# A list-scheduled attention and feed-forward kernel: other latency constants in its planner, and the tile table and side positions found under them

## The chip, the cores and the metric

The kernel runs on one core of one Trainium2 chip. The metric is the device time of one execution in microseconds (us): the median of several runs. Engines are named as the profile names them: PE (TensorE, matrix products), PEld (its weight loads), DVE (VectorE), ACT (ScalarE), POOL (GpSimd), SP (SyncE, which here issues the DMAs).

## What is computed

One layer-normalised input of 2048 rows by 512 columns goes through attention with 32 query heads of 16 columns and one shared key and value head, and in parallel through a feed-forward layer with GELU; both are added to the input.

```python
xn = _layernorm(x, axis=-1)
# attention: 32 heads, one k and one v head of 16 columns
scores = jnp.einsum("bhqd,bkd->bhqk", q, k) * (Dh ** -0.5)
p = _softmax(scores, axis=-1)
o = jnp.einsum("bhqk,bkd->bhqd", p, v)
# feed-forward: 512 -> 1792 -> 512
h = _gelu(jnp.einsum("bsd,df->bsf", x, w1) + b1)
return x + _A_ref(xn, ...) + _B_ref(xn, ...)
```

## The kernel before

**Tiles.** The score matrix is cut into 2048 tiles of 128 keys by 512 queries (one head each). Three tiles are a unit; there are 683 units. A unit's scores are made by PE in three of six PSUM banks (`scores`, L947); units alternate between the two halves of these six banks. Each tile then gets its exponential in one of two ways, and the string `DTAB` (L60) has one letter for each unit that says which of its three tiles goes which way.

- An exponential tile: ACT computes exp from PSUM into the buffer E (L970), one instruction for all such tiles of the unit, and PE multiplies it with V in one product (`pv_mm`, L1014).
- A spline tile: DVE makes a first pass from PSUM, add and max, into 16-bit integers Dt (L1001), whose bits read as bfloat16 are already a rough exponential. Three more shifted copies are made from it: two fast DVE instructions (L1047), the first over the batch, the second over twice the batch, and an in-place step of its own for each tile (L1044), which runs on POOL or on DVE. PE multiplies all five versions with V, so such a tile costs five products.

Spline tiles are collected in batches of one to six before the L1047 and L1044 steps. The letters `o`, `t`, `A`, `B`, `X` close the batch behind their unit; `0`, `2`, `a`, `b`, `x` do the same split without closing; `.` gives all three tiles to ACT. A batch also closes at six tiles and at the last spline tile of a group of 64.

**Other work.** Beside the units run the projections of the queries, the hidden layer of the feed-forward part (56 groups of products, evacuated by DVE at L1150), two GELU stretches on ACT (L1162, at units 182 and 512), the output products (`mm4`, L661) and the normalisation of the attention's output. `HP` and `YP` (L73, L74) hold the unit from which on each hidden group and each output tile may be planned.

**The planner.** Nothing of this order is written out by hand. The kernel first lists its operations with what they read and write, an assumed time on the engine (`occ`) and an assumed latency until another engine can go on (`lat`). `schedule` (L224) then plays all engines forward in time at build time and picks, for each engine that comes free, the ready operation with the earliest due time: that gives the fixed order of instructions of each engine. Waits between engines are semaphores, put in by `emit`; the planned times themselves don't reach the chip. `settle` (L457) works the times of the finished order out once more, and `emit` uses them to sort the waits of one instruction.

A POOL step has a rule of its own. DVE's fast operations (those marked `lock`) and POOL's are kept apart in the plan: when DVE starts an operation of at least `PL_WIN` (0.4) that isn't a fast one, a waiting POOL step may be placed in it, if POOL comes free within `PL_GATE` (0.1) of its start. The step is planned from `PL_START` after that start, lasts `PL_OCC` (0.62), can be used `PL_LAT` after its end, and fast DVE operations are barred until `PL_FREE` before its end:

```python
po.start = max(tt + PL_START, po.rdy, free["pool"])
po.end = po.start + po.occ
po.vis = po.end + po.lat
free["pool"] = tt = po.end
lockend = po.end - PL_FREE
```

A step that has been ready for `PL_TAKE` (1.0) may be taken by DVE instead, in its order of due times. `S_LAT` is the latency behind scores; DVE operations had 0.16, matrix products 0.23, exponentials 0.22.

Of the kernel before, what the change touches and what calls it, by code (L numbers as in the profile page):

```python
# [33 lines left out]
S_WAIT = 0.1  # L34
P_WAIT = 0.0
PL_OCC = 0.62
PL_LAT = 0.2
PL_GATE = 0.1
PL_WIN = 0.4
PL_TAKE = 1.0  # L40
PL_DUE = 3.0
PL_START = -0.07
PL_SEM = 0.16
PL_FREE = 0.135
NE_ND_KB = (23, 19, 11, 6)
LA = 34
LB = 120
# [9 lines left out]
DMASK = {".": (), "0": (0,), "2": (2,), "a": (0, 1), "b": (1, 2), "x": (0, 1, 2),  # L57
         "o": (0,), "t": (2,), "A": (0, 1), "B": (1, 2), "X": (0, 1, 2)}
CLOSE = "otABX"
DTAB = "t2t22t00202t..22tt..022.to00.t22t00200..o.t..20222o.o2.tot22.2t.t2222tt22..2o222t2..o202o02tt2.o.2.t0.t202.2.20t0toto.2..0ot.t2..ot0o2t02t.2222o.0t...o0ot2020o2.2t0.02.t00.02.20o002..xxXaoto.02oot.0to2tt.0too0.ot0tot.o0o020t0o0.tt20.t22.o0tto..2t2to220oo.22t0.2ooo.o2t2o.0ot0o.t02t022.to0..oot.2t2t.o0002ot.0.2tto.0tt2.02t0.202t.2t.oo.ot0.00t.t0o0.0o0o..o0o22o2.00.t0tot2.0o2.2o.t2o2o.tt22o.0t.0oo.2ot2t2.o0.t0t20to2.2t0t.tt2t.002tt.oo.o0oooo0.2o0o0.t00t2ot2.0t0tt0.oA.o..020tt2t02..t0000...2o..02ot0020o.t2t...00XbXttto200t.tt0o22tt..0t0t222.o2o2.t2t20.t0t0.t0t00t2o.0tt2tot.t000202t2t.o.0to20.0.2o22t0o.2t00o0t0..t02o0.0o.o0ooto.t2t0to.2oo0o222o0022o00.2t.2..t0t2.2t.tttt2.2.to.o.."  # L60
YF = 664
Y_ALLOW = 8.0
H_ALLOW = 5.0
YT_ALLOW = (3,3,3,3)
WF_ALLOW = 1.5
QP_ALLOW = 1.5
S_LAT = 0.27
S_REAL = 0.222
EXP_OCC = 0.0133
EXP_LAT = 0.16  # L70
Q3 = (7, 4, 2)
QK = ((48,88.7,157.4),(45,107.7,130.4),(62,118.7,159.4))
HP = ((14.33,26.29,49.54,147.27,14,38.77,51.6,14,34.61,92.18,56.17,130.88,103.7,49),(108.69,82.59,66.39,104.08,133,93.7,109.35,162.93,173.36,139,171.29,159.02,133,137.17),(308.62,328.89,290.1,325,306.98,336.81,316.24,310.73,293.91,381.46,369.7,349,374.48,453.6),(475,473.57,427,468.62,459.3,464.72,451,455.66,491.16,486.09,482.33,480.6,464.72,461.37))  # L73
YP = ((195.26,184.23,228.93,254.61),(353.39,411.43,387.54,421),(516,530.79,566.23,553.42),(600.53,607,655.32,660.47))  # L74
GU = ((182, (0, 1)), (512, (2, 3)))
FG = 7
UB2 = 2
# [13 lines left out]
NVA = 14  # L91
# [5 lines left out]
TBW = 512  # L97


def vcost(n, mode=1):  # L100
    return n / 0.96e3 / mode + 0.065
# [7 lines left out]
class Prog:  # L109
# [114 lines left out]
    def schedule(self):  # L224
# [17 lines left out]
        mode = None  # L242
# [6 lines left out]
        pend = 0.0  # L249
# [4 lines left out]
                accn[g] = accn.get(g, 0) + 1  # L254
        started = {}
        opened = None
        lockend, gate, prev = 0.0, None, None
        s_seen = False
        vleft = sum(op.kind == "v" for op in ops)
# [6 lines left out]
        while left:  # L266
# [11 lines left out]
            e, t = best_e, best_t  # L278
            cand = [o for o in able[e] if seen(o) <= t + 1e-9]
            if e == "pe":  # L280
                op = self.pick_pe(t, cand, ready["pe"], mode, visit, cgbusy)
# [8 lines left out]
                if op is None and self.pro_filler and not s_seen and low:  # L290
# [8 lines left out]
                    pend = st + f.occ  # L299
                    mode = "full"  # L300
# [13 lines left out]
                if FILL_GAP and tgt and low and st > FILL_FROM and lim - st > FILL_GAP:  # L314
# [12 lines left out]
                    pend = st + f.occ  # L327
                    mode = "col"
# [3 lines left out]
                if op == "idle":  # L332
                    op = None
# [4 lines left out]
            else:  # L338
                op = min(cand, key=self.due)
# [25 lines left out]
                if e == "dve" and op.kind == "pl":  # L365
                    ready["pool"].remove(op)
                    ready["dve"].append(op)
                    op.eng = op.stream = "dve"
                    op.kind, op.occ, op.lat = "post", vcost(TBW, 4), 0.16
                if e == "dve":  # L370
                    if op.lock:
                        gate = prev if prev is not None and t <= prev.end + 0.03 else op
# [7 lines left out]
            if e == "pe":  # L380
# [3 lines left out]
                if op.kind in ("pv", "side"):  # L384
                    cg = op.tag[1]
# [9 lines left out]
                    mode = "col"  # L395
                    g = op.tag[0]
                if op.kind == "pv":
                    n = accn[g] = accn[g] - 1
# [7 lines left out]
                elif op.kind != "side":  # L406
                    m = {"S": "row", "side": "col"}.get(op.kind, "full")
                    w = SWITCH if m != mode else 0.0
# [8 lines left out]
                    mode = m  # L417
# [4 lines left out]
            if e == "pe":  # L422
                while op.start > wend:
                    slow = 1.0 if area > HAM_T * WIN else 2.0
                    ncold += slow > 1
                    self.log.append((wend - WIN, area / WIN, slow))
                    area, wend = 0.0, wend + WIN
                pend = op.start + op.occ * slow
            free[e] = max(free[e], op.end)
            if op.pm:  # L430
                pmev = op if e == "dve" else None
# [5 lines left out]
            for o, cross in op.outs:  # L437
                o.nun -= 1
                v = op.vis if cross else op.end
# [8 lines left out]
        for op in order:  # L448
            if op.kind == "pv":
                g, cg, first = op.tag  # L450
# [5 lines left out]

    def settle(self):  # L457
        free = {e: 0.0 for e, _ in self.SECTIONS}
        mode, cg, pend = None, [0.0] * 4, 0.0
        for op in self.ops:  # L460
            occ = op.occ + EXP_OCC * (op.kind == "exp")
            lat = {"exp": EXP_LAT, "S": S_REAL, "fill": 0.0}.get(op.kind)
            lat = op.lat if lat is None else lat
            t = max([free[op.eng]] + [o.real for o in op.deps])
            if op.eng == "pe":
                if op.kind in ("pv", "side") or (op.kind == "fill" and occ > 0.15):
                    t = max(t, cg[op.tag[1]]) if mode == "col" else max([t, pend + SWITCH] + [c + SWITCH for c in cg])
                    cg[op.tag[1]] = t + 0.216
                    mode, end = "col", t + 0.006
                else:  # L470
                    m = "row" if op.kind == "S" else "full"
                    w = SWITCH if m != mode else 0.0
                    t = max([t, pend + w] + [c + w for c in cg])
                    mode, end = m, t + occ
                pend = t + occ
            else:
                end = t + occ
            free[op.eng] = max(free[op.eng], end)
            op.real = t + occ + lat

    def emit(self):
        self.settle()
# [44 lines left out]
def bass_parallel_sum__grouped_kv_mqa__dense_activation_gelu__prompt_kernel(  # L527
# [15 lines left out]
    S, D = xf.shape  # L543
# [17 lines left out]
    with ExitStack() as es:  # L561
# [76 lines left out]
        add = pr.add  # L638

        def B(b):  # L640
            return ("bank", b)

        def dve(fn, r=(), w=(), n=TBW, mode=1, allow=1.0, lat=0.16, **kw):
            return add("dve", fn, r, w, occ=vcost(n, mode), lat=lat, allow=allow, **kw)

        def act(fn, r=(), w=(), n=TBW, allow=0.0, lat=0.22, **kw):
            return add("act", fn, r, w, occ=0.051 + n / 1.2e3, lat=lat, allow=allow, **kw)
# [1 line left out]
        def mm(o, l, rh, start, stop, r=(), w=(), tp=None, skip=False, occ=0.216, allow=1.5, **ak):  # L649
            kw = {}  # L650
            if tp is not None:
                kw["tile_position"] = tp
            if skip:
                kw["skip_group_check"] = True
            return add("pe", lambda e: e.matmul(o, l, rh, start=start, stop=stop, **kw), r, w, occ=occ, lat=0.23,  # L655
                       allow=allow, **ak)

        def mm4(o, l, rh, start, stop, r=(), w=(), allow=1.5, **ak):
            for j in range(4):
                c = slice(32 * j, 32 * j + 32)  # L660
                add("pe", lambda e, c=c, j=j: e.matmul(o[c, :], l[:, c], rh, start=start, stop=stop,  # L661
                                                       tile_position=(0, 32 * j)),
                    r, [(k, j) for k in w] + [k for k in w if k != B(7)], occ=0.216, lat=0.23, allow=allow, kind="side", tag=(None, j), **ak)

        M4 = [(("bank", 7), j) for j in range(4)]

# [5 lines left out]
        for i in range(8):  # L672
            e = X_Q[i]
            dma("sp" if e == "s" else "act", x_sb[:, 2 * i:2 * i + 2, :], x_view[:, 2 * i:2 * i + 2, :], f"d_x{i}",
                w=[("x", 2 * i), ("x", 2 * i + 1)], lat=X_LAT[i], due=0.0)
# [6 lines left out]
        def setup(fn, r=(), w=(), occ=0.16, due=0.0, lat=0.1, **kw):  # L682
# [18 lines left out]
              w=[(k, g, j) for k in ("QT", "QTm") for g in range(NGR) for j in range(HG)])  # L701
        setup(lambda e: e.tensor_copy(wkp[:, :, :, 0:Dh], wvk[:, :, Dh:2 * Dh].unsqueeze(2).to_broadcast([P, DT, 4, Dh])),
              r=["wk_s", "wkp"], w=["wkp"], occ=0.35, due=2.0)
# [8 lines left out]
              r=["mrow"], w=["isc"], due=10.0)  # L712
# [10 lines left out]
        for gl in range(2):  # L723
            setup(lambda e, gl=gl: e.tensor_copy(sel_diag[gl], mask8[:, 4 * gl:4 * gl + 4].unsqueeze(1).to_broadcast([P, NGR // 2, HG])),
                  r=["mask8", "sel8"], w=["sel8"], due=12.0)
# [207 lines left out]
        def scores(u):  # L933
            ts = list(range(3 * u, min(3 * u + 3, NTILE)))
            x = u % 2
            pieces, r = [], []
            for i, t in enumerate(ts):
                gg, kt, j = tile_of(t)
                tb, g = divmod(gg, NGR)
                q0 = 32 * j  # L940
                pieces.append((bank(3 * x + i), KT[q0:q0 + 32, kt * P:(kt + 1) * P], QT[q0:q0 + 32, g, :], q0))
                r.append(("KT", kt))
                r += [k for k in q_rows(g) if k not in r]

            def fn(e):
                for o, l, rh, q0 in pieces:
                    ins = e.matmul(o, l, rh, start=True, stop=True, tile_position=(q0, 0))  # L947
                return ins
            return add("pe", fn, r, [B(3 * x + i) for i in range(len(ts))], occ=0.216, lat=S_LAT, allow=-1.0, kind="S")

# [62 lines left out]
        def pv_mm(gg, j, v, kt, rhs, r):  # L1013
            add("pe", lambda e, a, b: e.matmul(pO[32 * j:32 * j + 32, :], V1[:, v, kt, :], rhs, start=a, stop=b,  # L1014
                                               tile_position=(0, 32 * j)),
                r=r + [("V", v, 0 if kt < NVA else NVA)], acc="O", occ=0.216, lat=0.23,
                allow=4.0 if gg < NTB * NGR - 1 or kt < NT - 4 else -5.0, kind="pv", tag=(gg, j))

        def close_batch():
# [198 lines left out]
        side = []  # L1218
# [40 lines left out]
        for t in range(NTILE):  # L1259
            if is_d[t]:  # L1260
                first, n = (t, 1) if n == 0 else (first, n + 1)
                if n == KB or last_d[t // TPG] == t or (DTAB[t // 3] in CLOSE and not any(is_d[t + 1:t // 3 * 3 + 3])):
                    bsize[first], n = n, 0

        scores(0)
        scores(1)
        for u in range(NU):
# [89 lines left out]
```

## Time and profile before

| what | value |
|---|---|
| median of 3 runs | 750.98 us (750.9 to 751.15) |
| the profiled execution | 750.71 us |
| its span in the profile | 749.0 us |
| PE, DVE, ACT busy | 98% each |
| POOL busy | 364.4 us, 49% |
| first first-pass and first exponential start | 24.09 us |
| last exponential starts | 738.61 us |
| TensorE clock granted | 0.998 |

A row of the profile's groups reads: line, engine, operation, output and input with their shapes, count, then busy time and the mean of one instruction, then the engine's idle time ahead of such instructions and what ended it. The share of busy time is an average over records, and a record of DVE or ACT runs on while the next instruction has begun: to see how long an instruction holds its engine, one takes the distance from its start to the next one's.

### The profile page before, as it was taken

What the parts mean: (1) busy time and instruction counts of PE and PEld (TensorE: products, weight loads), DVE (VectorE), ACT (ScalarE), POOL (GpSimd) and SP (SyncE); (2) the same over time, 40 slices, a digit from 0 to 9 for tenths busy, and PEclk for the clock granted to TensorE, in tenths of its full rate; (3) what the DMA queues carried; (4) which work ended last, traced back from release to release, by engine and by line L of the source; (5) the groups of instructions that cost most, each with busy time, mean ns of one, the idle gap of its engine ahead of it and who ended that gap; (6) DMA issues with size and microseconds to landing.
All of it is one profiled execution on the core that took longest, in us unless ns stands there. A gap on an engine that the chain in (4) does not pass through costs nothing.

```text
span 749.0 us, 21922 instructions
## 1 busy us (share of the span) xinstructions
PE 732.8 (98%) x9046; PEld 228.2 (30%) x9046; DVE 736.1 (98%) x1436; ACT 733.2 (98%) x744; POOL 364.4 (49%) x506
## 2 busy tenths in 40 slices
PE   7999999999999999999999999999999999999998
PEld 4323222222233323232222222332233333322223
DVE  8899999999999999999999999999999999999996
ACT  8999999999999999999999999999999999999995
POOL 5443654343523576554546555553452466454441
PEclk9999999999999999999999999999999999999999
DMA  9200100000011011100101010100100101010101
GB/s 315 61 15 17 32 9 17 24 11 21 6 36 25 9 39 30 24 23 16 26 13 28 17 38 19 29 24 16 25 15 22 40 6 41 23 39 10 25 22 37
DMA packets 32077, 23.34 MB, mean 31 GB/s; under 512 B 16369, under 2 KB 27498, under 8 KB 31978
## 3 DMA queue, kind: packets, MB, share of 16 engines
q1 hardware_dynamic: 30922, 21.90, 10.9%
q8 instruction: 72, 1.18, 0.7%
q14 instruction: 27, 0.22, 0.1%
q10 hardware_dynamic: 1056, 0.03, 0.1%
HBM read 13.08 MB, written 2.35 MB: 21 GB/s over the span
## 4 chain that ended last, share of the span: by engine, by line
PE 40%; DVE 30%; ACT 28%; DMA 0%; issue 0%; SPq 0%
ACT E L970 28%; PE pAll L1014 19%; DVE Dt L1001 13%; PE pAll L947 13%; DVE Dt L1047 10%; PE pAll L661 7%; DVE x_sb L1150 2%; DVE stats L748 1%; DVE Dt L1044 1%; DVE Of L1059 1%; PE pAll L655 1%; DMA x_sb<-in_A_x_dram 0%; DVE oTp L1086 0%; DVE qp L1122 0%; DVE x_sb L1196 0%
## 5 line engine op out<-in xcount | busy, mean ns | idle before, releaser
L970 ACT ACTIVATE E<-pAll 128x1024 bf16<-128x1024 f32 (+1 forms) x678 | 682.4, 1226 | 1.7 <-PE pAll L947 1.2
L1044 POOL TENSOR_SCALAR Dt<-Dt 128x512 int16<-128x512 int16 x451 | 348.2, 772 | 360.6 <-DVE Dt L1047 143.8
L1014 PE MATMUL pAll<-Dt,V 128*32 128x512 bf16 x2775 | 421.8, 383 | 0.6 <-DVE Dt L1047 0.2
L1001 DVE TENSOR_SCALAR Dt<-pAll 128x512 int16<-128x512 f32 (+1 forms) x542 | 364.1, 688 | 1.0 <-PE pAll L947 0.8
L1047 DVE TENSOR_SCALAR Dt<-Dt 128x1024 int16<-128x1024 int16 (+7 forms) x548 | 288.0, 551 | 0.2
L1014 PE MATMUL pAll<-E,V 128*32 128x512 bf16 x1493 | 284.8, 385 | 0.2
L947 PE MATMUL pAll<-QT,KT 32*128 32x512 bf16 x2048 | 267.2, 384 | 6.2 <-ACT E L970 2.1
L947 PEld LDWEIGHTS pAll<-QT,KT 32*128 32x128 bf16 x2048 | 67.3, 91 | 279.5 <-ACT E L970 251.4
L1014 PEld LDWEIGHTS pAll<-Dt,V 128*32 128x32 bf16 x2775 | 110.9, 94 | 119.4 <-issue 72.0
L661 PE MATMUL pAll<-xnT,w_sb 128*32 128x512 bf16 x896 | 122.2, 383 | 0.4 <-DVE x_sb L1150 0.3
L1014 PEld LDWEIGHTS pAll<-E,V 128*32 128x32 bf16 x1493 | 65.9, 94 | 47.5 <-issue 34.7
L661 PE MATMUL pAll<-w_sb,x_sb 128*32 128x512 bf16 x448 | 69.3, 383 | 0.0
L661 PE MATMUL pAll<-w_sb,ub 128*32 128x512 bf16 x448 | 69.3, 383 | 0.0
L661 PE MATMUL pAll<-wop,oTp 128*32 128x512 bf16 x256 | 49.5, 383 | 0.0
L661 PEld LDWEIGHTS pAll<-xnT,w_sb 128*32 128x32 bf16 x896 | 32.1, 95 | 22.4 <-issue 11.8
L1044 DVE TENSOR_SCALAR Dt<-Dt 128x512 int16<-128x512 int16 x104 | 26.7, 279 | 0.0
L661 PE MATMUL pAll<-xnT,wq_sb 128*32 128x512 bf16 x256 | 22.5, 383 | 0.0
L1150 DVE TENSOR_SCALAR x_sb<-pAll,b1T 128x512 bf16<-128x512 f32 x28 | 20.6, 736 | 0.7 <-PE pAll L661 0.6
L1059 DVE COPY Of<-pAll 128x512 f32<-128x512 f32 x31 | 20.9, 674 | 0.0
L1150 DVE TENSOR_SCALAR ub<-pAll,b1T 128x512 bf16<-128x512 f32 x28 | 20.6, 736 | 0.0
L661 PEld LDWEIGHTS pAll<-w_sb,x_sb 128*32 128x32 bf16 x448 | 17.1, 94 | 8.8 <-issue 7.0
L661 PEld LDWEIGHTS pAll<-w_sb,ub 128*32 128x32 bf16 x448 | 17.6, 94 | 4.7 <-issue 2.9
(121 smaller groups left out, 254.6 us busy)
## 6 DMA issues: line engine op xcount, KB each, us to landing
OfP<-Of SPq DMA_DIRECT2D x124, 32.0 KB, 1.9
rbP<-rden_rows SPq DMA_DIRECT2D x124, 32.0 KB, 1.8
w_sb<-in_B_w_dram SPq DMA_DIRECT2D x2, 1792.0 KB, 12.7
x_sb<-in_A_x_dram SPq DMA_DIRECT2D x8, 256.0 KB, 4.3
x_sb<-in_A_x_dram SPq DMA_DIRECT2D x16, 128.0 KB, 2.2
QT<-qp SPq DMA_DIRECT2D x124, 16.0 KB, 1.8
out_dram<-x_sb SPq DMA_DIRECT2D x12, 128.0 KB, 1.7
wq_sb<-in_A_wq_dram SPq DMA_DIRECT2D x1, 512.0 KB, 6.2
```

Of the source, the lines that this page charges most:

```text
L655: return add("pe", lambda e: e.matmul(o, l, rh, start=start, stop=stop, **kw), r, w, occ=occ, lat=0.23, allow=allow, **ak)
L661: add("pe", lambda e, c=c, j=j: e.matmul(o[c, :], l[:, c], rh, start=start, stop=stop, tile_position=(0, 32 * j)), r, [(k, j) for k in w] ...
L748: dve(lambda e, ti=ti, c=c: e.bn_stats(stats[:, c, :], x_sb[:, ti, :]), r=[("x", ti)], w=[("st", ti)], n=511, due=land(ti) + DU["sd"])
L947: ins = e.matmul(o, l, rh, start=True, stop=True, tile_position=(q0, 0))
L970: o = act(lambda e: e.activation(E[:, s0:s0 + na, :], bank(b0, na).rearrange("p (a n) -> p a n", a=na), ACT.Exp, scale=LN2 / 128.0), w=[B( ...
L1001: op = dve(lambda e: e.tensor_scalar(Dt[:, s:s + n, :], bank(bk, n).rearrange("p (a n) -> p a n", a=n), float(127 * 128) + SPL_D, SPL_MIN, ...
L1014: add("pe", lambda e, a, b: e.matmul(pO[32 * j:32 * j + 32, :], V1[:, v, kt, :], rhs, start=a, stop=b, tile_position=(0, 32 * j)), r=r + [ ...
L1044: add("pool", lambda e, d=d, k=k: e.tensor_scalar(d, d, 1.0, float(k), ALU.mult, ALU.add), [], [(("D", base[o > 0] + q), o)], occ=PL_OCC, ...
L1047: dve(lambda e, d=view(o, nb), q=view(i, nb), k=k: e.tensor_scalar(d, q, float(k), None, ALU.add), r=keys(i), w=keys(o), n=nb * n * TBW, m ...
L1059: dve(lambda e: e.tensor_copy(Of[:, i, :], pO), w=["O", ("Of", i)], allow=0.0)
L1150: dve(lambda e: e.tensor_scalar(ubs[tb % 2][:, ft, :], pM, b1T[:, ft:ft + 1], None, ALU.add), r=["b1T"], w=M4 + [ukey(tb, ft)], n=TBW + 57 ...
```

## The change

The planner's constants are replaced: the latency behind scores (`S_LAT`), behind DVE operations and matrix products (0.16 and 0.23 become `D_LAT` and `P_LAT` from the first unit on; the prologue keeps the old values), behind exponentials (a lag that grows by `A_INC` for each exponential that follows another without a break), and the place, latency and bar of a POOL step. `DTAB`, `HP` and `YP` are other values, found by a search with these constants. No operation's code changes, and the number of spline tiles is the same.

```diff
--- before
+++ after
@@ constants
-PL_LAT = 0.2
+PL_LAT = 0.06
...
-PL_START = -0.07
+PL_START = 0.065
 PL_SEM = 0.16
-PL_FREE = 0.135
+PL_FREE = 0.06
...
-DTAB = "t2t22t00202t..22tt..022.to00.t22t00200..o.t..20222o.o2.tot22.2t.t2222tt22..2o222t2..o202o02tt2.o.2.t0.t202.2.20t0toto.2..0ot.t2..ot0o2t02t.2222o.0t...o0ot2020o2.2t0.02.t00.02.20o002..xxXaoto.02oot.0to2tt.0too0.ot0tot.o0o020t0o0.tt20.t22.o0tto..2t2to220oo.22t0.2ooo.o2t2o.0ot0o.t02t022.to0..oot.2t2t.o0002ot.0.2tto.0tt2.02t0.202t.2t.oo.ot0.00t.t0o0.0o0o..o0o22o2.00.t0tot2.0o2.2o.t2o2o.tt22o.0t.0oo.2ot2t2.o0.t0t20to2.2t0t.tt2t.002tt.oo.o0oooo0.2o0o0.t00t2ot2.0t0tt0.oA.o..020tt2t02..t0000...2o..02ot0020o.t2t...00XbXttto200t.tt0o22tt..0t0t222.o2o2.t2t20.t0t0.t0t00t2o.0tt2tot.t000202t2t.o.0to20.0.2o22t0o.2t00o0t0..t02o0.0o.o0ooto.t2t0to.2oo0o222o0022o00.2t.2..t0t2.2t.tttt2.2.to.o.."
+DTAB = "2oo222to.o2.t22.t02.t22t.2.ot0t.to02t2o.0o..22220t.2.0oo0t0.o02.t.t002t2.0.t.tt0t00t.2o202ttt...2t00.o22o.2222o2..20o0o0t.0oo2..t02020o00..to0022t.0..20t0o2o..00t0t.0t.tt2o.0.2tot222.xXxA.2tto.ottt0.2o0tot.20oto.22t00o02o.oo00o0.0o2.02.t02t.o20t2o22to0.o2.t202.t0o.22t0020o0.t22.0t.0.oot2.o2o0o.0t2o..22o20.t20o..2t2t.2o.00ooo.00o..t2t.t020.20.0o00.o020.t.0to22t.o002o.0t.2o0t2t2o.0o.02t0t0o2.tt2t222.oo..2t2200.o0t0.t00o.o0o0.2o0o20.too.00t02t.20.2oo020o0.20t.t.too0o.t2.2002o.o00t.2o.oto..tt22..t22t2.t222.2t..bXaXoBot02o000t22o.2t..022o20t.t22t.2o0202.22o.0oto2t.22o20..o2o0tt0.2oot00t2.t0o0t.02o.200t.tto02ot.o000.2.o2.tt0t.2o0o0t.tto2oo22020o2t0t..2o0.tt..0t220oo0o.02.o2.2t.o.."
...
-S_LAT = 0.27
-S_REAL = 0.222
-EXP_OCC = 0.0133
-EXP_LAT = 0.16
+S_LAT = 0.217
+A_LAG = 0.113
+A_INC = 0.0125
+A_SEM = 0.056
+D_LAT = 0.135
+P_LAT = 0.217
...
-HP = ((14.33,26.29,49.54,147.27,14,38.77,51.6,14,34.61,92.18,56.17,130.88,103.7,49),(108.69,82.59,66.39,104.08,133,93.7,109.35,162.93,173.36,139,171.29,159.02,133,137.17),(308.62,328.89,290.1,325,306.98,336.81,316.24,310.73,293.91,381.46,369.7,349,374.48,453.6),(475,473.57,427,468.62,459.3,464.72,451,455.66,491.16,486.09,482.33,480.6,464.72,461.37))
-YP = ((195.26,184.23,228.93,254.61),(353.39,411.43,387.54,421),(516,530.79,566.23,553.42),(600.53,607,655.32,660.47))
+HP = ((16.96,14,48.27,139.83,19.95,35.9,58,14.3,43.94,90.38,48.92,127.17,90.44,77.53),(110.87,61.1,60.99,112,144.58,144.53,130,86.34,135.21,163.06,164.65,178,148.03,100),(295.91,306.95,295.3,312.61,302.48,302.82,304,324.94,322,334,346,286,336.14,473.45),(472.85,489.16,431.92,491.13,437.6,470.94,459.13,467.63,498.84,496.01,496.23,487.59,461.81,465.31))
+YP = ((184,183.11,202.23,226.81),(346,403.6,370,421.81),(517.2,529.33,580,561.85),(600,614.37,652,653.91))
@@ schedule
+        aend = 0.0
...
-                    op.kind, op.occ, op.lat = "post", vcost(TBW, 4), 0.16
+                    op.kind, op.occ, op.lat = "post", vcost(TBW, 4), D_LAT
...
+            if e == "act" and op.kind in ("exp", "gelu"):
+                aend = max(op.end + A_LAG, aend + op.occ + A_INC)
+                op.vis = aend + A_SEM
@@ settle
-            occ = op.occ + EXP_OCC * (op.kind == "exp")
-            lat = {"exp": EXP_LAT, "S": S_REAL, "fill": 0.0}.get(op.kind)
-            lat = op.lat if lat is None else lat
+            occ = op.occ
+            lat = 0.0 if op.kind == "fill" else op.lat
...
+            if op.kind in ("exp", "gelu"):
+                aend = max(end + A_LAG, aend + occ + A_INC)
+                op.real = aend + A_SEM
@@ the kernel's helpers
-        def dve(fn, r=(), w=(), n=TBW, mode=1, allow=1.0, lat=0.16, **kw):
-            return add("dve", fn, r, w, occ=vcost(n, mode), lat=lat, allow=allow, **kw)
+        dlat = [0.16, 0.23]
+
+        def dve(fn, r=(), w=(), n=TBW, mode=1, allow=1.0, **kw):
+            return add("dve", fn, r, w, occ=vcost(n, mode), lat=dlat[0], allow=allow, **kw)
...
+        dlat[:] = D_LAT, P_LAT
         scores(0)
         scores(1)
```

More of the change, by code (lines that the diff above doesn't have):

```diff
@@ L458, in settle @@
         free = {e: 0.0 for e, _ in self.SECTIONS}
-        mode, cg, pend = None, [0.0] * 4, 0.0
+        mode, cg, pend, aend = None, [0.0] * 4, 0.0, 0.0
         for op in self.ops:
-            occ = op.occ + EXP_OCC * (op.kind == "exp")
-            lat = {"exp": EXP_LAT, "S": S_REAL, "fill": 0.0}.get(op.kind)
-            lat = op.lat if lat is None else lat
+            occ = op.occ
+            lat = 0.0 if op.kind == "fill" else op.lat
             t = max([free[op.eng]] + [o.real for o in op.deps])
@@ L654, in mm @@
                 kw["skip_group_check"] = True
-            return add("pe", lambda e: e.matmul(o, l, rh, start=start, stop=stop, **kw), r, w, occ=occ, lat=0.23,
+            return add("pe", lambda e: e.matmul(o, l, rh, start=start, stop=stop, **kw), r, w, occ=occ, lat=dlat[1],
                        allow=allow, **ak)
@@ L662, in mm4 @@
                                                        tile_position=(0, 32 * j)),
-                    r, [(k, j) for k in w] + [k for k in w if k != B(7)], occ=0.216, lat=0.23, allow=allow, kind="side", tag=(None, j), **ak)
+                    r, [(k, j) for k in w] + [k for k in w if k != B(7)], occ=0.216, lat=dlat[1], allow=allow, kind="side", tag=(None, j), **ak)
         M4 = [(("bank", 7), j) for j in range(4)]
@@ L1015, in pv_mm @@
                                                tile_position=(0, 32 * j)),
-                r=r + [("V", v, 0 if kt < NVA else NVA)], acc="O", occ=0.216, lat=0.23,
+                r=r + [("V", v, 0 if kt < NVA else NVA)], acc="O", occ=0.216, lat=dlat[1],
                 allow=4.0 if gg < NTB * NGR - 1 or kt < NT - 4 else -5.0, kind="pv", tag=(gg, j))
```

## The prediction

> **What bounds the kernel now.** I read the page first: span, busy time per engine.
>
> ```profile
> span 749.0 us, 21922 instructions
> ...
> PE 732.8 (98%) x9046; PEld 228.2 (30%) x9046; DVE 736.1 (98%) x1436; ACT 733.2 (98%) x744; POOL 364.4 (49%) x506
> ```
>
> Three engines at 98% do not say which one is full, because records overlap: an instruction's record runs on while the next has begun. So I went to the time-ordered view, VectorE alone, around 307 us, and read starts instead of durations (columns: start, duration, engine and line).
>
> ```profile
> 307.17 0.68 DVE L1001 TENSOR_SCALAR Dt<-pAll 128x512 int16<-128x512 f32 x1
> 307.76 0.41 DVE L1047 TENSOR_SCALAR Dt<-Dt 128x1024 int16<-128x1024 int16 x1
> 308.10 0.68 DVE L1001 TENSOR_SCALAR Dt<-pAll 128x512 int16<-128x512 f32 x1
> 308.70 0.41 DVE L1047 TENSOR_SCALAR Dt<-Dt 128x1024 int16<-128x1024 int16 x1
> 309.03 0.68 DVE L1001 TENSOR_SCALAR Dt<-pAll 128x512 int16<-128x512 f32 x1
> ```
>
> A first pass (L1001) holds VectorE 0.60 us, not 0.68, a step over 1024 elements (L1047) 0.33 us, not 0.41. I took these start-to-start times for every instruction between 30 and 735 us. On VectorE they hardly vary: 600 ns mean for 527 first passes (median 600). Summing what exceeds the usual time of each shape, VectorE loses 5.2 us between its first first-pass (24.1 us) and its last in-place step (738.8 us). ScalarE's two-bank exponentials have a floor of 904 ns and a mean of 924: 10.6 us lost over 527 of them, about 13 us with the three-bank ones and GELU. Hence **VectorE is the full engine**, ScalarE has some 13 us of slack that its records hide, and the time is 24.1 prologue + 709.5 VectorE work + 5.2 waits + 10.2 tail (738.8 to 749.0) = 749.0. The wait list agrees that no long wait stands ahead of either:
>
> ```profile
> POOL Dt L1044 <- DVE Dt L1047: 143.8, 85, 10.1
> ...
> ACT E L970 <- PE pAll L947: 1.2, 2, 0.7
> ...
> DVE Dt L1001 <- PE pAll L947: 0.8, 2, 0.4
> ```
>
> VectorE waits 0.8 us in two places for scores; the long waits are GpSimd's (POOL), which is busy 49% and ends nothing. Then the groups by shape, for the counts:
>
> ```profile
> L1001 DVE TENSOR_SCALAR Dt<-pAll 128x512 int16<-128x512 f32 x534 | 352.2, 675 | 1.0 <-PE pAll L947 0.8
> L1044 POOL TENSOR_SCALAR Dt<-Dt 128x512 int16<-128x512 int16 x451 | 348.2, 772 | 360.6 <-DVE Dt L1047 143.8 <-PE pAll L1014 93.6 <-DVE Dt L1001 46.2
> ...
> L1047 DVE TENSOR_SCALAR Dt<-Dt 128x1024 int16<-128x1024 int16 x204 | 82.2, 414 | 0.1
> L1047 DVE TENSOR_SCALAR Dt<-Dt 128x2048 int16<-128x2048 int16 x105 | 71.2, 680 | 0.0
> ...
> L1044 DVE TENSOR_SCALAR Dt<-Dt 128x512 int16<-128x512 int16 x104 | 26.7, 279 | 0.0
> ```
>
> 555 in-place steps (L1044), one for each tile that VectorE takes: 451 ran on POOL, 104 on VectorE.
>
> **The change, part by part.**
>
> *Table.* Counting letters of both tables through the masks: 555 spline tiles and 1493 exponential tiles before and after. So PV products (5 x 555 + 1493 = 4268), elements of every kind and ScalarE's count (678) stay. Its shapes go from 535 two-bank, 140 three-bank, 3 one-bank to 533, 141, 4: -2 x 0.904 + 1.331 + 0.494 = +0.02 us, nothing. First passes go from 542 to 541 (one more of two tiles). What moves is where a batch closes: 274 batches become 258 (of one tile 116 to 91, of three 38 to 54). Each batch is two L1047 instructions over the same total of elements, so 548 become 516. Start to start, 1024 elements take 0.334 us and 2048 take 0.600: 0.266 for 1024 elements, leaving 0.068 fixed. 33 instructions less: 33 x 0.068 = **-2.2 us** on the full engine, all of it on the path.
>
> [...]
>
> *In-place steps.* Which engine takes one decides 0.202 us of VectorE each. Matching the 555 starts in order with the batches, VectorE took 14% of those from one-tile batches, 12% for two, 20% for three, 22, 36 and 33% for four, five, six. The new batch counts (91, 84, 54, 16, 8, 5) by these shares give 105 against 104: **0 us**. Bounds: 52 more (rival C) at +10.5; none left on VectorE at -21, which nothing supports, as POOL idles mostly because no work is ready for it. I take 0, the row nearest, with 10 steps (2.0 us) either way as the forecast's own width.
>
> *Latency constants.* They set the planned order and carry no time to the chip, where instructions wait on semaphores. They come closer to this trace: matrix loads start 0.729 us after a first pass starts (38 cases), 0.131 after its 0.598 (planned 0.16, now 0.135); exponentials that waited start 0.431 after their scores, 0.215 after 0.216 (0.27, now 0.217); a load follows a POOL step's end by 0.05 (0.2, now 0.06). So a plan with less air: 0 us taken, bounded by VectorE's 5.2 us of waits below and by doubling them above.
>
> *POOL constants.* The plan now starts a POOL step 0.065 after VectorE's instruction instead of 0.07 before it, ends it at 0.685, and bars fast VectorE steps until 0.625. The trace has the POOL step end 0.556 after that instruction's start (median), and the fast step behind a first pass start at 0.598 whether POOL runs (51 cases) or not (218). So the bar of 0.027 per step, up to 451 x 0.027 = 12 us, exists in the plan alone; no semaphore carries it. Its cost is 0 as long as the order still has VectorE's next input ready; without that cover it is rival B.
>
> Of 633 fast steps, 61 began with a POOL step still running; 14 of these were held back, 1.8 us in all. [...]
>
> *Side positions.* 56 hidden-layer groups, 16 output tiles: same instructions, other places. The last hidden group moves from unit 173.4 to 178 ahead of the GELU at 182, and from 491.2 to 498.8 ahead of 512. ScalarE waits 1.3 us in two places for such a group (its last GELU quarter); 4.6 units later at 1.05 us a unit could add up to 4.8 us there, covered by ScalarE's 13 us of slack: 0.
>
> *Sum* against the profiled execution: 750.71 (span 749.0 + 1.7 around it) - 2.2 = 748.5. The median shown is 750.98, 0.27 above that execution: **748.8 us**.
>
> **Rivals.**
>
> *A, waits shrink too.* The third POOL step of a run of first passes is no longer placed (C), so the 14 meetings go, and truer latencies trim waits: -1.8 more, 747.0; with 8 fewer in-place steps on VectorE (1.6) 745.4. For it: all constants but POOL's start move towards the trace. Against: VectorE waits so little already.
>
> *B, the saving is swallowed.* ScalarE and VectorE work one ring of six score banks. With 2.2 us less, VectorE comes within some 6 us of ScalarE's floor, and an order that was planned with 12 us of imaginary bars can leave it waiting for scores. Then 0.8 us of such waits becomes about 3: 751.0, no change.
>
> *C, slower: VectorE gets the in-place steps.* In the plan, a POOL step in each of three first passes in a row ended at 0.55, 1.17, 1.79, each within 0.1 of the next slot (0.598, 1.196). Now the ends are 0.685 and 1.305, and 1.305 is over 1.196 + 0.1: the third is refused. In the trace 171 of 450 POOL steps start within 0.1 us of the one before; runs of three or more hold 157, a third is 52. Should half, 26, fall to VectorE: 26 x 0.202 = +5.3, 754.1. It decides from 11 steps more (gain gone), 18 for over 0.2% slower. Against: most displaced steps find the next slot, as POOL is idle half the time.
>
> *That the change doesn't do what it says* is excluded for the table, whose counts are certain; for the latencies it is B.
>
> **How the numbers follow.** Forecast 0.46 (748.8, own range 746.8 to 750.8), A 0.12, B 0.17, C 0.25. A measurement of this kernel can tell about 0.2% (1.5 us) from no change, so faster means below 749.5: 0.35 of the forecast's 0.46, and A: 0.47. Within: the other 0.11, and B: 0.28. Slower: C, 0.25. The range goes from A's lower price, 745.4, to C's, 754.1; beyond lie half of C and a part of A, under 2 in 10.
>
> **What would show it.** Right: 516 L1047 and 541 L1001 rows, 95 to 115 L1044 rows on VectorE, first passes still 0.60 start to start, VectorE's stretch of 714.7 us shorter by about 2, prologue and tail as now. Wrong: over 115 L1044 rows on VectorE (C); first passes or exponentials that wait on L947 in total for over 3 us (B); a GELU quarter that waits over 3 us; a tail longer than 10.2 us because PV products are left over when the last exponential ends, which no term here covers.

## The result, and the profile after

The changed kernel takes 749.44 us (median of 14 runs, 749.22 to 749.61) against 750.98 us before (14 runs beside them): the ratio is 0.998 with a 95% interval of 0.9972 to 0.9988, 1.5 us or 0.2% faster. The forecast was 748.8. The profiled execution has a span of 747.5 us, 1.5 less than before. Its page (busy time per engine, then the chain that ended last, by engine):

```profile
span 747.5 us, 21851 instructions
...
PE 730.1 (98%) x9038; PEld 223.4 (30%) x9038; DVE 734.0 (98%) x1392; ACT 732.0 (98%) x744; POOL 367.9 (49%) x517
...
ACT 77%; PE 14%; DVE 8%; DMA 0%; issue 0%; SPq 0%
```

The busy shares are the same five numbers. The chain isn't; the same line of the page before, which the prediction left out, was

```profile
PE 40%; DVE 30%; ACT 28%; DMA 0%; issue 0%; SPq 0%
```

The groups by shape of the changed kernel (all line numbers are 10 higher than before) show the counts:

```profile
L1011 DVE TENSOR_SCALAR Dt<-pAll 128x512 int16<-128x512 f32 x532 | 353.4, 680 | 2.6 <-PE pAll L957 1.5
L1054 POOL TENSOR_SCALAR Dt<-Dt 128x512 int16<-128x512 int16 x462 | 351.3, 760 | 355.8 <-DVE Dt L1057 175.0 <-DVE Dt L1011 57.3 <-PE pAll L1024 55.1
...
L1057 DVE TENSOR_SCALAR Dt<-Dt 128x1024 int16<-128x1024 int16 x175 | 71.4, 417 | 0.1
L1057 DVE TENSOR_SCALAR Dt<-Dt 128x2048 int16<-128x2048 int16 x100 | 67.9, 681 | 0.0
...
L1054 DVE TENSOR_SCALAR Dt<-Dt 128x512 int16<-128x512 int16 x93 | 24.4, 281 | 0.0
```

541 first passes and 516 fast steps, as counted from the table; 93 in-place steps on VectorE, where 105 were expected and 104 had been. So VectorE's work fell by more than forecast, and the time by less. Start to start, each shape against the quickest quarter of both kernels, VectorE's stretch reads:

| | first first-pass | work | waits | rest to the end | sum |
|---|---|---|---|---|---|
| before | 24.1 | 708.1 | 6.3 | 10.5 | 749.0 |
| after | 24.3 | 703.8 | 9.6 | 9.9 | 747.5 |

4.3 us of work went, 3.3 us of waits came: a first pass that follows a first pass lost 0.7 us in all before and 3.4 us after. The waits list has the beginning of it (waits, times, longest):

```profile
ACT E L980 <- PE pAll L957: 2.3, 5, 0.5
...
DVE Dt L1011 <- PE pAll L957: 1.5, 3, 0.8
```

Such lines show only idle time between records; most of the 9.6 us lies under records that run on. The question is then why 4.3 us less work on an engine that was called full gave only 1.5 us.

### The profile page after: what moved, and what is told of

Read it like the earlier page. It is cut to its first block, busy times and chain, and to the rows that moved or that the text cites. A ratio compares the mean times of both kernels' runs of the same rounds, so it can differ in the third digit from the quotient of the medians.

```text
span 747.5 us, 21851 instructions
## 1 busy us (share of the span) xinstructions
PE 730.1 (98%) x9038; PEld 223.4 (30%) x9038; DVE 734.0 (98%) x1392; ACT 732.0 (98%) x744; POOL 367.9 (49%) x517
## 4 chain that ended last, share of the span: by engine, by line
ACT 77%; PE 14%; DVE 8%; DMA 0%; issue 0%; SPq 0%
ACT E L980 76%; PE pAll L1024 6%; PE pAll L957 4%; PE pAll L671 3%; DVE Dt L1011 3%; DVE Dt L1057 2%; DVE stats L758 1%; DVE x_sb L1160 1%; DMA x_sb<-in_A_x_dram 0%; PE pAll L665 0%; DVE ub L794 0%; ACT xnT L814 0%; DVE qp L1132 0%; PE pAll L1329 0%; ACT ub L791 0%
## 5 line engine op out<-in xcount | busy, mean ns | idle before, releaser
L1024 PE MATMUL pAll<-E,V 128*32 128x512 bf16 x1493 | 280.7, 385 | 0.0
L1024 PEld LDWEIGHTS pAll<-Dt,V 128*32 128x32 bf16 x2775 | 109.1, 94 | 117.8 <-issue 75.0
L671 PE MATMUL pAll<-xnT,w_sb 128*32 128x512 bf16 x896 | 119.8, 383 | 1.6 <-DVE x_sb L1160 1.6
L671 PE MATMUL pAll<-w_sb,ub 128*32 128x512 bf16 x448 | 66.4, 382 | 0.0
L671 PE MATMUL pAll<-wop,oTp 128*32 128x512 bf16 x256 | 45.2, 382 | 0.0
L1054 DVE TENSOR_SCALAR Dt<-Dt 128x512 int16<-128x512 int16 x93 | 24.4, 281 | 0.0
## 6 DMA issues: line engine op xcount, KB each, us to landing
w_sb<-in_B_w_dram SPq DMA_DIRECT2D x2, 1792.0 KB, 12.7
```

The source lines that it names most:

```text
L1054: add("pool", lambda e, d=d, k=k: e.tensor_scalar(d, d, 1.0, float(k), ALU.mult, ALU.add), [], [(("D", base[o > 0] + q), o)], occ=PL_OCC, ...
```

## The experiments

Theory 1 is the prediction's: VectorE sets the time, each us of its work shows. Theory 2 is that VectorE and ScalarE wait on each other through the six score banks, so that a third shows. Theory 3 was formed after the first four runs: ScalarE sets the time, once it is counted from end to end. Each ratio is to the kernel before, run beside it; after itself stands at 0.998.

**Constants alone** (the changed kernel with the tables of before):

```diff
-DTAB, HP, YP of after
+DTAB, HP, YP of before
```

> The changed kernel with the tile table and the side positions of before: the constants alone. The program has 548 L1057 steps, 542 first passes and 185 in-place steps on VectorE (before 104, after 93). Theory 1 (VectorE's work decides, 0.202 us for each in-place step): 81 steps more than before are 16.4 us, so 751.0 + 16.4 = 767 us. Theory 2 (the ring of score banks decides, and VectorE's work shows in the time by a third only, as 4.3 us less work gave 1.5 us from before to after): 751.0 + 5.5 = 756.5 us. If truer latencies shorten waits by themselves, either comes out lower by up to 6 us.

Measured 795.24 us, ratio 1.0592 (1.0570 to 1.0614). Both theories are far off: 81 in-place steps explain 16 of 44 us. What ScalarE waited for:

```profile
ACT E L980 <- PE pAll L1024: 23.1, 10, 5.9
ACT x_sb L1172 <- DVE x_sb L1160: 9.9, 3, 5.6
ACT ub L1172 <- DVE ub L1160: 7.6, 1, 7.6
```

Exponentials wait until PV products have read their place in E, and GELU parts for hidden groups that come late.

**Tables alone** (the kernel before with the new tables):

```diff
-DTAB, HP, YP of before
+DTAB, HP, YP of after
```

> The kernel before with the tile table and side positions of after: the tables alone, old constants. The program has 516 L1047 steps, 541 first passes and 166 in-place steps on VectorE. Theory 1: -2.2 us for 33 instructions less, +12.5 us for 62 in-place steps more than before: 761.3 us. Theory 2, a third of that: 754.4 us.

Measured 776.30 us, 1.0338 (1.0323 to 1.0354), again beyond both theories: 62 in-place steps more explain 12.5 of 25 us. Neither half is worth anything by itself: the tables fit one plan, and either half alone makes another.

**Shorter first passes** (order unchanged; the same edit, with 24 or 8 columns, serves three runs):

```diff
+            c = TBW - CUT_D if all(i in full for i in range(s, s + n)) else TBW
+            full.update(range(s, s + n))
-            op = dve(lambda e: e.tensor_scalar(Dt[:, s:s + n, :], bank(bk, n).rearrange(...),
+            op = dve(lambda e: e.tensor_scalar(Dt[:, s:s + n, 0:c], bank(bk, n).rearrange(...)[:, :, 0:c],
```

> The changed kernel, order and waits unchanged, but the first pass of a tile leaves out the last 24 of its 512 columns once its place in Dt has been written in full, which leaves that part of the spline tiles stale: about 520 x 25 ns = 13 us less work on VectorE, nothing else. Theory 1 (VectorE sets the time): -10 to -13 us, 736 to 739 us. Theory 2 (VectorE and ScalarE wait on each other through the score banks, a third shows): -4 us, 745 us; the rest turns into first passes that wait for scores.

Measured 748.29 us, 0.9967 (0.9955 to 0.9979): 1.1 us for 13. Theory 1 falls for the changed kernel, and theory 2's third is too much.

**Shorter exponentials** (order unchanged):

```diff
+                c = TBW - CUT_A if all(i in fullE for i in range(s0, s0 + na)) else TBW
+                fullE.update(range(s0, s0 + na))
-                o = act(lambda e: e.activation(E[:, s0:s0 + na, :], bank(b0, na).rearrange(...),
+                o = act(lambda e: e.activation(E[:, s0:s0 + na, 0:c], bank(b0, na).rearrange(...)[:, :, 0:c],
```

> The changed kernel, order and waits unchanged, but the exponentials leave out the last 12 of 512 columns of each tile once its place in E has been written in full (that part is stale): about 1470 x 10 ns = 14.7 us less work on ScalarE, nothing on VectorE. Theory 1: within 1 us of 749.4, since ScalarE has slack. Theory 2: -3 to -5 us, 745 us, with VectorE's waits for scores falling from 9.6 us in its stretch towards 5.

Measured 743.67 us, 0.9904 (0.9890 to 0.9919): 5.8 us. VectorE's waits fell from 9.6 to 4.3 us. In the changed kernel the engine said to have 13 us of slack is the one that counts. With these exponentials the chain that ended last has left ScalarE:

```profile
PE 63%; DVE 27%; ACT 9%; issue 1%; DMA 0%; SPq 0%
```

Why the slack was none is seen in ScalarE's time-ordered rows of the changed kernel. Each row merges an exponential with the one after it (start, time to the end of the second):

```profile
134.85 2.17 ACT L980 ACTIVATE E<-pAll 128x1024 bf16<-128x1024 f32 x2
...
135.75 2.19 ACT L980 ACTIVATE E<-pAll 128x1024 bf16<-128x1024 f32 x2
...
136.66 2.20 ACT L980 ACTIVATE E<-pAll 128x1024 bf16<-128x1024 f32 x2
```

Starts are 0.90 apart, ends 137.02, 137.94, 138.86, so 0.92 apart. While starts are so, each record is 12 to 13 ns longer than the one before; then one start comes later (by 0.12 us at 137.68, by 0.06 us at 144.04), and the next record is short again (1.17 us both times). From end to end the steps are 0.916 (1024 elements) and 1.343 us (1536), nearly every one. Counted so, ScalarE from its first exponential's end to its last has 708.9 us of work in both kernels and waits of 5.7 us before and 4.1 us after: 25.1 + 708.9 + 5.7 + 9.3 = 749.0, and 25.3 + 708.9 + 4.1 + 9.2 = 747.5. That is theory 3.

The chain in order of time shows the same. Before, its two long stretches of exponentials alone were

```profile
26.70 68.85 ACT E L970 x68
...
290.77 139.19 ACT E L970 x138
```

and after

```profile
56.79 149.40 ACT E L980 x147
...
229.54 288.45 ACT E L980 x288
...
572.07 130.20 ACT E L980 x132
```

By this chain, ScalarE's own pace alone set the time in 208 us before and in 568 us after.

**Shorter first passes in the kernel before**, by 24 and by 8 columns:

> The kernel before, order and waits unchanged, its first passes leaving out the last 24 of 512 columns of a tile once its place in Dt has been written in full (stale there): some 13 us less work on VectorE. Theory 1 (VectorE sets the time of the kernel before): 738 to 741 us. Theory 3 (ScalarE sets it: counted from end to end its exponentials take 0.917 and 1.343 us, 708.4 us of a stretch of 714.6, so 6.2 us of waits are all that is to be had): 748 to 750 us.

Measured 748.36 us, 0.9965 (0.9951 to 0.9978): 2.8 us for 13, as theory 3 has it.

> The kernel before, order and waits unchanged, first passes without the last 8 of 512 columns once written in full (stale there): some 4.4 us less work on VectorE, as much as the change took off it, without the change's order. If lighter work on VectorE is what made the change faster, at ScalarE's waits' cost: 749.4 us, the time of after. If it is the order: 750.5 to 751. Theory 1 in its plain form (every us of VectorE shows): 746.5 us.

Measured 749.21 us, 0.9975 (0.9965 to 0.9985): 1.9 us for 4.3, no less than the whole change. So a lighter VectorE can make a gain of this size. It is not the same gain: counted from end to end, ScalarE's waits fell by 1.5 us at exponentials and by 0.3 at GELU here, and by 0.5 and 1.1 in the change. Whether the lighter VectorE made the change's gain is asked the other way round.

**More work for VectorE, order unchanged**:

```diff
+            npad[0] += 1
+            pd = npad[0] % 8 == 0
+            def p1_fn(e, s=s, n=n, bk=bk, pd=pd):
+                if pd:
+                    e.memset(pad_t[:, 0:4], 0.0)
+                return e.tensor_scalar(Dt[:, s:s + n, :], ...)
```

> The changed kernel, order unchanged, with a VectorE memset of 4 elements ahead of every eighth first pass: 67 instructions of some 0.066 us, 4.4 us more work on VectorE, which gives back what the change took off it. Theory 1: 753.8 us. If the lighter VectorE made the gain: 750.9 us, the time of before. If the order made it: 749.4 to 750 us.

Measured 749.61 us, 0.9979 (0.9970 to 0.9989). Inconclusive: the 0.066 us was my estimate, which no run had shown, and the trace has the 67 memsets hold VectorE for a median of 14 ns each. With 48 columns instead of 4:

> The changed kernel, order unchanged, with a memset of 48 columns on VectorE ahead of every eighth first pass. (With 4 columns the same memset held VectorE by some 16 ns only, 1 us in all, so that run settled nothing.) At 48 elements I expect 0.05 to 0.08 us each, 67 of them 3.5 to 5 us, which gives back the 4.3 us that the change took off VectorE. Theory 1 (VectorE sets the time): 753 to 754 us. Theory 3 (ScalarE sets it; VectorE shows only in ScalarE's waits), with the lighter VectorE as the cause of the gain: 750.5 to 751 us. Theory 3 with the new order as the cause: 749.5 to 750 us.

Measured 749.28 us, 0.9981 (0.9972 to 0.9990). The time doesn't move, but the work wasn't added either. One place with the memset, then the same place in the changed kernel without it (start, duration):

```profile
63.24 0.41 DVE L1066 TENSOR_SCALAR Dt<-Dt 128x1024 int16<-128x1024 int16 x1
63.61 0.10 DVE L1018 MEMSET pad_t<- 128x48 f32 x1
63.63 0.63 DVE L1019 TENSOR_SCALAR Dt<-pAll 128x512 int16<-128x512 f32 x1
64.19 0.41 DVE L1142 TENSOR_TENSOR sqq<-qp 128x512 bf16<-128x512 bf16 x1
```

```profile
63.28 0.41 DVE L1057 TENSOR_SCALAR Dt<-Dt 128x1024 int16<-128x1024 int16 x1
63.61 0.68 DVE L1011 TENSOR_SCALAR Dt<-pAll 128x512 int16<-128x512 f32 x1
64.21 0.41 DVE L1133 TENSOR_TENSOR sqq<-qp 128x512 bf16<-128x512 bf16 x1
```

From the first row's start to the last row's are 0.95 and 0.93 us. Over the 67 places, the memset makes the first pass behind it start 57 ns later, and that first pass then holds VectorE 47 ns less (medians, each place against the same place without the memset). What is left is 11 ns, 0.6 us in all, as with 4 columns. So neither run gave back the 4.3 us, and neither tells whether VectorE's lighter work or the new order made the gain. The chain stays ScalarE's, 77%.

**More work for ScalarE, order unchanged**:

```diff
+                npad[0] += 1
+                pd = npad[0] % 10 == 0
+                def exp_fn(e, s0=s0, na=na, b0=b0, pd=pd):
+                    if pd:
+                        e.activation(pad_t[:], xnT[:, 0, 0:48], ACT.Copy)
+                    return e.activation(E[:, s0:s0 + na, :], ..., ACT.Exp, scale=LN2 / 128.0)
```

> The changed kernel, order unchanged, with a small copy (48 columns) on ScalarE ahead of every tenth exponential, 67 in all, 0.05 to 0.1 us each, 3.5 to 7 us more work on ScalarE, none on VectorE. Theory 1 (ScalarE has 12 us of slack): 749.4 to 750.5 us. Theory 3 (ScalarE is full from end to end): nearly every us shows, 752.5 to 756 us, as many us as the trace shows between the ends.

Measured 756.84 us, 1.0081 (1.0067 to 1.0095). The page and the group of the copies:

```profile
span 755.0 us, 21918 instructions
```

```profile
L987 ACT ACTIVATE pad_t<-xnT 128x48 f32<-128x48 bf16 x67 | 24.4, 364 | 0.0
```

The mean record is 364 ns, but from end to end a copy adds 0.12 us (median), also when counted to the end of the fifth instruction behind it. That is some 8 us for all 67, and the span rose by 7.5. So nearly every us added on ScalarE shows, while of 13 us taken off VectorE in the same order 1.1 showed. For the changed kernel theory 1 is out and theory 3 stands.

**Shorter exponentials in the kernel before** (the edit as above):

> The kernel before, order and waits unchanged, exponentials without the last 12 of 512 columns once their place in E has been written in full (stale there): 14.7 us less work on ScalarE. In the changed kernel the same cut gave 5.8 us and left VectorE with 4.3 us of waits. Theory 3 with VectorE close behind ScalarE: here VectorE's own work is 4.3 us longer, so it gives 4.3 us less, about 1.5 to 2.5 us: 748.5 to 749.5 us. Were ScalarE the only engine that counts: 736 us. Theory 1: 750 to 751 us, nothing.

Measured 749.75 us, 0.9986 (0.9976 to 0.9995): 0.9 us, where the same edit gave the changed kernel 5.8. The chain:

```profile
PE 54%; DVE 42%; ACT 3%; issue 1%; DMA 0%; SPq 0%; POOL 0%
```

With ScalarE relieved by the same amount in both, the changed kernel is 0.9904 / 0.9986 = 0.992 of the one before, some 6 us. This is where the rest of the change went: the chain of PE and VectorE, which stood 1 us behind ScalarE before, was cut by some 6 us, and all but 1.5 us of that is hidden behind ScalarE's own work. In the kernel before no engine set the time alone: 14.7 us off ScalarE gave 0.9, and 13 us off VectorE gave 2.8.

**More work for VectorE in the kernel before** (the memsets of 48 columns):

> The kernel before, order unchanged, with a memset of 48 columns on VectorE ahead of every eighth first pass: 67 times 0.059 us as the trace of the same padding in the changed kernel showed, 4.0 us more work on VectorE. In the changed kernel that cost nothing. Theory 3 with VectorE close behind ScalarE in the kernel before (its cut of 4.3 us gave 1.9 us, and 14.7 us less on ScalarE gave only 0.9 us): 2 to 4 us, 752.7 to 754.7 us. If the kernel before has as much room on VectorE as the changed one: 751 us, nothing. Theory 1: 4 us, 754.7 us.

Measured 751.45 us, 1.0005 (0.9996 to 1.0014): between nothing and 1 us, less than I expected. But the 4.0 us of the expectation weren't added: here too the first pass behind a memset holds VectorE 46 ns less, so that a memset adds 12 ns, 0.8 us in all. ScalarE's waits rose by about 0.5 us. How much more work VectorE could take in the kernel before, this run doesn't tell.

**The old POOL constants in the changed kernel**:

```diff
-PL_START = 0.065; PL_LAT = 0.06; PL_FREE = 0.06
+PL_START = -0.07; PL_LAT = 0.2; PL_FREE = 0.135
```

> The changed kernel with the old three constants of the POOL steps (-0.07, 0.2, 0.135), new latencies, tables and side positions. The program has 156 in-place steps on VectorE, 63 more than after. Theory 1: 63 x 0.202 = 12.7 us more, 762 us. Theory 3: the tables fit only the plan they were found under, and what is lost is ScalarE waiting (GELU parts and scores that come late), more than VectorE's work explains: 770 to 785 us, with over 25 us of end-to-end waits on ScalarE.

Measured 781.48 us (one run). Where it lost, by the waits list:

```profile
ACT x_sb L1172 <- DVE x_sb L1160: 18.1, 3, 10.4
...
ACT E L980 <- PE pAll L957: 5.1, 9, 1.0
```

GELU stands 18.1 us in three places for hidden groups. As expected of theory 3, ScalarE's stretch grew by 28.7 us, all of it waits from end to end, of the 32 us lost; the tail has the rest. VectorE's 63 in-place steps (12.7 us) are less than half of it.

## Why the prediction was near, and where it was wrong

- *"VectorE is the full engine, ScalarE has some 13 us of slack": wrong, and the step that failed.* ScalarE was read start to start, floor 904 ns; its real step is 916 ns, visible only between ends. Some 8 of the 13 us were its own work. What contradicts it are the copies on ScalarE (7.5 us for some 8 in the changed kernel) beside the shorter first passes on VectorE (1.1 us for 13 there, 2.8 for 13 in the kernel before). The chain by engine, with ScalarE in it at 28%, spoke against it and wasn't used.
- *33 instructions less, -2.2 us: the counts were right, the work term too, its place on the path wrong.* VectorE's work fell by 4.3 us, by 2.2 for these and 2.2 for 11 in-place steps, and the time fell by 1.5, as ScalarE's waits fell by 1.6. With VectorE lighter by as much in the old order, 1.9 showed. So half of the saved work was foreseen and about a third of it showed; that the forecast's 2.2 and the measured 1.5 lie close is chance.
- *In-place steps, 0 with 10 either way: 11 fewer.* The shares by batch size fell for five of six sizes (14 to 10% for one tile, 33 to 23% for six).
- *Latency and POOL constants cost nothing by themselves: true for what runs on the chip, but the orders they give differ by far more than the bounds set.* Constants alone cost 44 us, tables alone 25. The plan and its tables are one object; a bound from VectorE's waits could not have held a part of it.
- *Side positions, 0: probably mis-sized.* From end to end GELU's parts lost 1.7 us before and 0.6 us after, 1.1 of the 1.6 us gained. No run separates the positions from the rest of the change, and a lighter VectorE alone took 0.3 us off these waits. The later positions, which were thought to cost up to 4.8 us, show no cost; the waits list has 1.3 us in two places before and now

```profile
ACT x_sb L1172 <- DVE x_sb L1160: 0.3, 1, 0.3
```

- *Rival A's meetings* of fast steps with a running POOL step: 14 delayed for 1.7 us before, 8 for 0.6 after. In the changed kernel 63 fast steps began while a POOL step ran (61 before, by the same count), so most of these were not held back. *Rival C* didn't come in the whole change: POOL's runs of three or more hold 130 steps, 157 before, and it took 462 in all. That steps can fall to VectorE is real: 156 to 185 did where plan and tables didn't match. But 156 and 166 of these were under the old POOL constants, so the refused third step, its mechanism, isn't shown.
- *Rival B* had the right shape, VectorE's saving turned into waits for scores. ScalarE is a cause of them, as they fell from 9.6 to 4.3 us with shorter exponentials; what the plan's imaginary bars add, no run separates.

Open: whether VectorE's lighter work, the new order or the side positions took the 1.6 us off ScalarE's waits. A lighter VectorE alone can give as much, but at exponentials rather than at GELU, and no run put the 4.3 us back in the new order. PE, also busy 98%, was neither lightened nor padded by itself.

## What to carry to other kernels

When several engines are at 98%, count each one end to end as well as start to start before calling one of them full (here the same exponentials end 0.916 us apart and start 0.904 apart), and read the chain by engine beside it. What the busy shares left open here was settled for the changed kernel by a few padded or shortened instructions on one engine, order unchanged. Read from the trace what they really added, counted past the instruction behind the padding: here a first pass gave back 47 of the 57 ns by which a memset had delayed it. This scheduler's constants and the tables found under them couldn't be priced apart: alone they cost 44 and 25 us, together they gained 1.5. And of the change's work on the engines that weren't the longest only 1.5 us showed; with ScalarE's exponentials shortened alike in both kernels it was some 6 us.

## What the runs showed of the hardware that was not expected

- Exponentials from PSUM start every 0.904 us and end every 0.916 (1024 elements, in both kernels); while they start so, the records grow by 12 to 13 ns each until a start slips. From 1024 to 1536 elements the slope is (1331 - 904) / 512 = 0.834 ns an element. Estimated from it, starts show 904 - 854 = 50 ns beyond the elements' own time, and ends show 62 ns. It is the ends that the time follows here: copies that added some 8 us between ends made the span 7.5 us longer.
- A copy of 48 columns on ScalarE, ahead of an exponential of the changed kernel, has a record of 364 ns (mean of 67) and adds 0.12 us from end to end (median).
- A memset of 48 columns ahead of a first pass has a record of 98 ns and makes the first pass start 57 ns later, but that first pass then holds VectorE 0.55 us instead of 0.60. So the memset adds 11 ns, no more than one of 4 columns does (14 ns, record 62 ns).
